# Gated mix of sliding-window attention and a SwiGLU feed-forward: one feed-forward tile by block products instead of two, a new deal of slots, and V's first quarter in another order

## The chip, the core and the metric

The kernel runs on one core of a Trainium2 chip. The metric is the device time of one launch in microseconds (us). The core's engines work side by side, each through its own list of instructions: TensorE (PE in the profile, with its weight loads as PEld), VectorE (DVE), ScalarE (ACT), GpSimd (POOL) and SyncE (SP), which issues most of the transfers (DMAs).

## What is computed

The input x has 2048 rows of 512 numbers. The output mixes two branches by a gate per row:

```python
g = _sigmoid((x * gate_w).sum(-1, keepdims=True))
a = _A_ref(x, A_wqkv, A_wo)                        # attention, 32 heads of 16, row q sees rows q-255 .. q
b = (_silu(x @ w_gate) * (x @ w_up)) @ w_down      # feed-forward, 1792 hidden columns
return g * a + (1 - g) * b
```

## The kernel before, in words

**Numbers.** Every large product is made with each operand split into a high part and a low part (`split`, L67), and three matmuls stand for one: high x high, high x low, low x high. A matmul has 512 moving columns as a rule. The 512 contraction rows are four slices (k = 0 to 3) of 128, so a sum of 128 x 512 results takes 12 matmuls of 128 rows.

**Stages.** TensorE goes through these in order:

1. *V* (L145 to L286). x arrives in four chunks of 512 rows, each in four slices, on SyncE's queue; the four slices of V's weights on ScalarE's queue. Each slice is split: the high part on ScalarE, the low part on VectorE for x, and for V's weights on VectorE (k = 0) or GpSimd (the others), L173 to L178, with two fills of V's store (`fill_v`, L165) on GpSimd among them. The first four row blocks of V (the first quarter) are made together in four accumulators (`first`, L214): for each k, for each of the four row blocks, the three products of that slice (L215 to L217). The other twelve row blocks follow one by one.
2. *Block products* (L367 to L436). Queries and keys of eight groups of four heads, taken in four pairs of groups, and gate and up of the first `NSF` feed-forward tiles (a tile is 128 of the 1792 hidden columns), one tile a pair. In a pair, the two by two blocks of weights and x are combined by additions so that seven block products do what eight would; for the two halves of the rows that makes 7 x 2 x 6 = 84 matmuls of 128 rows. Query and key results are split and written to DRAM (`xd`), gate and up are written as they are (`raws`, L335). In the last pair the constant rows of the first query and key stores are filled and the first heads' queries and keys are read back (`stack`, L320).
3. *The streams beside attention* (L484 to L841). Gate and up of all the other tiles are made by `stream` (L580): the list `UNITS` (L107) has two units, gate and up, a tile, and each unit has four sums, one a chunk of x. The first unit runs alone with whole matmuls (`whole`, L514: 48 steps, one matmul each). The others run in two *lanes* (`lanes`, L525): each sum's contraction is cut into halves of 64 rows, lane 0 does the upper half of a sum, lane 1 the lower half of it, 18 steps later. A *step* is one half matmul of 64 rows in either lane; the two lanes lie in different row halves of the array. 12 steps is the worth of one sum. A finished sum is copied by ScalarE (`copy_out`, L508) and written to `raws`. When a unit is done, the next weights but one are split (`prepare`, L299: the high part on ScalarE, the low part on GpSimd).
   Attention's own work is cut into *slots*. First come 64 slots with the first score pass of head group 0 and three steps each (L690). Then come 128 *blocks* of four slots (L812): in a slot, one head of the first score pass for a later group (`stage1`, L591: a score matmul of 63 rows, whose masked maximum VectorE takes) and one head of the second pass (`stage2`, L631: a score matmul of 64 rows, its exponential by ScalarE, L644, and the masks on GpSimd), then as many steps as the list `DEAL` (L805) says for that block's place in its round of four blocks, dealt out over the four slots. At the second slot of a round's first block stand the value products of the round before (`av`, L654) and their evacuation (`evacuate`, L669). From block 112 on (the last head group, 16 blocks) there is no first score pass any more, and the second list of `DEAL` counts. There the first two feed-forward tiles are also prepared for the last stage: their gate and up are read back (`tile_load`, L740) and go through `tile_early` (L745) on ScalarE and VectorE, at fixed slots; the down weights are split on VectorE.
4. *The last stage* (L843 on): the down product of the feed-forward branch over 14 tiles and four chunks, with the output product of attention between.

The order on each engine is the order of the program, written out by hand; nothing reorders it. What `later`, `at`, `soft` and `spread` hold is tied to slots (for `soft`, copies of finished sums just before value products are put behind them). The matmuls of the score passes rotate through PSUM banks that VectorE (first pass) or ScalarE (second pass) must have read before; the streams rotate through three banks of their own.

Of the kernel before, what the change touches and what calls it, by code (L numbers as in the profile page):

```python
# [12 lines left out]
ALU = mybir.AluOpType  # L13
# [5 lines left out]
NK = D // P  # L19
# [14 lines left out]
def gated_mix(ctx, tc, xT, xn, wqk, wv, wo, wgu, wd, gw, out):  # L34
# [4 lines left out]
    nc = tc.nc  # L39
# [27 lines left out]
    def split(hi, lo, src, hi_eng, lo_eng):  # L67
        if hi_eng is nc.scalar:
            nc.scalar.copy(hi, src)
        else:  # L70
            hi_eng.tensor_copy(hi, src)
        lo_eng.tensor_tensor(out=lo, in0=src, in1=hi.bitcast(F32), op=ALU.subtract)
# [14 lines left out]
    def run(gen, n=None):  # L87

        while n is None or n > 0:
            if next(gen, run) is run:  # L90
                break
            n = n and n - 1
# [10 lines left out]
    def weights_of(key):  # L103
        return wqk[key[1]] if key[0] == "p" else wgu[key[1], :, key[2]]

    NSF = 2
    UNITS = [("f", f, i) for f in range(NSF, NF) for i in range(2)]  # L107

    psum = ctx.enter_context(tc.tile_pool(name="psum", bufs=1, space=PSUM))
# [2 lines left out]
    def bank(n):  # L112
        names = BANKS[n if isinstance(n, str) else ("pa", "pb", "pc", "pd")[n]]
        names.append(names.pop(0))
        return psum.tile([P, CH], F32, name=names[-1])
# [7 lines left out]
    wvh = vpool.tile([P, NK, D], F32R, name="wvh")  # L123
    wvl = vpool.tile([P, NK, D], F32R, name="wvl")
    vs = [vpool.tile([P, G, 2, VW], F32, name=f"vs{i}") for i in range(2)]

    def pair_fetch(keys):
        raw = wide.tile([P, 4, 2 * P], F32, name="rw")
        for i, key in enumerate(keys):
            nc.sync.dma_start(by_k(raw[:, 2 * i:2 * i + 2].rearrange("p a n -> p (a n)")), weights_of(key))  # L130
        return raw

    def u_tile():
        return wide.tile([P, CH], F32, name="u", bufs=6)
# [6 lines left out]
    def xk(c, k):  # L141
        return halves_of(xraw[2 * c + k // 2])[k % 2]

    wvraw = [u_tile() for _ in range(NK)]
# [6 lines left out]
    PAIRS = [(("p", g), ("p", g + 1)) for g in range(0, G, 2)]  # L151
    PAIRS += [(("f", f, 0), ("f", f, 1)) for f in range(NSF)]
    RW = {0: pair_fetch(PAIRS[0])}
# [11 lines left out]
    def fill_v(t):  # L165
        nc.gpsimd.memset(t, 0.0)
        for i in range(2):
            nc.gpsimd.memset(t[:, :, i, :68].rearrange("p g (j e) -> p g j e", e=17)[:, :, :, DH], 1.0)

    def split_x(c, k):  # L170
        split(xhi[c][:, k], xlo[c][:, k], xk(c, k), nc.scalar, nc.vector)

    for k in range(NK):  # L173
        split_x(0, k)
        split(wvh[:, k], wvl[:, k], wvraw[k], nc.scalar, nc.vector if k == 0 else nc.gpsimd)
        if k == 1:
            fill_v(vs[0])
    fill_v(vs[1])  # L178

    def v_products(b):  # L180
        c, o = divmod(b * P, CH)
        return [(xt[c][:, k, o:o + P], wt[:, k]) for k in range(NK)
                for xt, wt in ((xhi, wvh), (xhi, wvl), (xlo, wvh))]
# [24 lines left out]
    def vproj(b, ps, ks=range(NK)):  # L208
        todo = v_products(b)
        for k in ks:  # L210
            for n in range(3 * k, 3 * k + 3):
                nc.tensor.matmul(ps, *todo[n], start=n == 0, stop=n == 3 * NK - 1)

    first = [bank(n // 2) for n in range(4)]  # L214
    for k in range(NK):  # L215
        for b in range(4):
            vproj(b, first[b], (k,))  # L217
    for c in (1, 2):
# [250 lines left out]
    with ExitStack() as A:  # L469
# [121 lines left out]
        def stage1(g, qb):  # L591

            hf, b = divmod(qb, NB // 2)
            if b == 0:
                MX[g, hf] = sm.tile([P, 4, NB // 2], F32, name="mx")
            q0, k0 = qb * P, max(0, qb - 2) * P
            n = q0 + P - k0
            for hd in range(4):
                pr, j = divmod(hd, 2)
                r = slice(64 * j, 64 * j + 63)  # L600

                ps = bank("pd") if g == 0 and pr else bank("pc")
                nc.tensor.matmul(ps[:, :n], QT[g % 2][pr][r, q0:q0 + P], KT[g % 2][pr][r, k0:k0 + n],  # L603
                                 start=True, stop=True)
                mx = nc.vector.tensor_tensor_reduce(out=ps[:, :n], in0=ps[:, :n], in1=mask[:, 3 * P - n:],  # L605
                                                    scale=1.0, scalar=NEG, op0=ALU.add, op1=ALU.max,
                                                    accum_out=MX[g, hf][:, hd, b:b + 1])
                if g == 0:
                    BEHIND.append(mx)
                yield  # L610
# [76 lines left out]
        first = chain(*(stage1(0, b) for b in range(NB)))  # L687
# [114 lines left out]
            spread(4 * (16 * g + 9) + 3, 1, stack(g + 2, 0))  # L802
            spread(4 * (16 * g + 17) + 1, 1, stack(g + 2, 1))

        DEAL = [[[(hd + 1) * n // 4 - hd * n // 4 for hd in range(4)] for n in deal] for deal in ((5, 9, 8, 8), (8, 8, 8, 8))]  # L805
        DEAL[0][0] = 1, 2, 2, 0
        scores = chain(*(stage1(*divmod(b, NB)) for b in range(NB, G * NB)))
        run(scores, 1)
        for t in range(G * NB + 1):
# [7 lines left out]
            for hd in range(4):  # L817
                k = NOW[0] = NSLOT * t + hd
# [8 lines left out]
                if t < G * NB:  # L827
                    run(steps, DEAL[t >= g7][part][hd])
                if hd == 1 and values:
# [205 lines left out]
```

## Time and profile before

| what | us |
|---|---|
| median of 3 runs | 823.76 (821.94 to 824.28) |
| the profiled execution | 822.11 |
| its span, first to last instruction | 820.4 |
| stages in the profiled execution: block products from | 50.66 |
| the streams from | 164.90 |
| blocks of four slots from | 216.13 |
| the last group of heads (block 112) from | 568.38 |
| the last stage from | 619.46 |

How to read it: the profile shows one execution. A line like L564 is a line of the kernel above: L564 are the half matmuls of the lanes, L603 and L642 the two score passes, L664 the value products, L381 the block products, L212 V. A group or a timeline row names what is written and read (`pa<-xhi,wh`: into a bank of pool pa, from the high part of x and of a weight). A bracket at the end of a row gives the idle time before it and what ended it. Matmuls overlap, so a matmul's length is not its price: the distance between the starts of two that follow each other in the same rows of the array is.

### The profile page before, as it was taken

To read this page: it belongs to the slowest core of one execution; us is meant where nothing else is said; L and a number is where in the kernel's file an instruction comes from. 1 tells how busy PE (TensorE), PEld (TensorE's weight loads), DVE (VectorE), ACT (ScalarE), POOL (GpSimd) and SP (SyncE) were. 2 spreads that over 40 slices of the span, in tenths; PEclk is the share of its full clock that TensorE was granted. 3 is DMA by queue.
4 is the path that set the end of the run, shared out by engine and by line. 5 is a ranking of instruction groups with operands and counts; after the bars stand their busy time and mean duration, and the time that the engine had idled before them with its cause. 6 is when DMAs were issued, how large, how long until landed. Compare 5 with 4: busy or idle time off the path is not lost.

```text
span 820.4 us, 20498 instructions
## 1 busy us (share of the span) xinstructions
PE 812.0 (99%) x7681; PEld 681.0 (83%) x7681; DVE 550.4 (67%) x1425; ACT 470.0 (57%) x956; POOL 402.1 (49%) x715
## 2 busy tenths in 40 slices
PE   9999999999999999999999999999999999999997
PEld 7888888878888888888888888888887888888886
DVE  5675554248877888878888887786576666554652
ACT  7455553312576767767677676776776563435340
POOL 5124442260366666767667576665873205442320
PEclk9999999999999999999999999999999999999999
DMA  8446666385625654566555655352659997878611
GB/s 302 148 156 254 231 231 235 137 268 178 218 85 194 189 179 157 182 213 202 171 167 168 207 188 159 132 170 89 212 191 349 271 287 229 273 226 221 213 52 52
DMA packets 80211, 159.70 MB, mean 195 GB/s; under 512 B 14960, under 2 KB 19440, under 8 KB 80112
## 3 DMA queue, kind: packets, MB, share of 16 engines
q1 hardware_dynamic: 68544, 127.44, 47.5%
q0 software_dynamic: 10992, 29.91, 11.3%
q8 instruction: 60, 0.98, 0.5%
q10 hardware_dynamic: 576, 1.05, 0.4%
q14 instruction: 39, 0.32, 0.1%
HBM read 93.32 MB, written 65.01 MB: 193 GB/s over the span
## 4 chain that ended last, share of the span: by engine, by line
PE 95%; DMA 2%; DVE 1%; ACT 1%; POOL 0%; SPq 0%; issue 0%; DVEq 0%; ACTq 0%
PE pa L564 22%; PE pb L564 10%; PE pd L642 6%; PE pc L664 5%; PE pd L381 4%; PE pb L381 4%; PE pa L381 4%; PE pd L81 3%; PE pc L81 3%; PE pc L83 3%; PE pd L83 3%; PE pc L82 3%; PE pd L82 3%; PE pb L664 2%; PE pc L381 2%; PE pb L83 2%
## 5 line engine op out<-in xcount | busy, mean ns | idle before, releaser
L644 ACT ACTIVATE pt<-pd 128x384 f32<-128x384 f32 (+2 forms) x491 | 223.0, 474 | 43.9 <-PE pd L642 25.6
L605 DVE CUSTOM_DVE_ANT_0 pc<-pc,mask 128x384 f32<-128x384 f32 (+2 forms) x322 | 173.2, 548 | 23.5 <-PE pc L603 9.6
L642 PE MATMUL pd<-q,k 64*128 64x384 f32 (+2 forms) x491 | 167.2, 348 | 1.8 <-ACT pt L644 1.8
L564 PE MATMUL pa<-xhi,wh 64*128 64x512 f32 x492 | 168.5, 395 | 0.0
L564 PE MATMUL pa<-xlo,wh 64*128 64x512 f32 x492 | 167.6, 394 | 0.0
L564 PE MATMUL pa<-xhi,wl 64*128 64x512 f32 x492 | 165.9, 395 | 0.0
L646 POOL TENSOR_SCALAR_AFFINE_SELECT pt<-pt 128x256 f32<-128x256 f32 x256 | 110.9, 434 | 67.9 <-ACT pt L644 62.7
L642 PEld LDWEIGHTS pd<-q,k 64*128 64x128 f32 x491 | 90.8, 185 | 26.1 <-ACT pt L644 9.8
L603 PE MATMUL pc<-k,q 63*128 63x384 f32 (+2 forms) x322 | 106.9, 337 | 0.0
L564 PE MATMUL pb<-xhi,wl 64*128 64x512 f32 x244 | 96.2, 394 | 0.0
L564 PE MATMUL pb<-xhi,wh 64*128 64x512 f32 x244 | 96.2, 394 | 0.0
L564 PE MATMUL pb<-xlo,wh 64*128 64x512 f32 x244 | 96.2, 394 | 0.0
L649 POOL TENSOR_SCALAR_AFFINE_SELECT pt<-pt 128x256 f32<-128x256 f32 x224 | 94.3, 421 | 0.0
L605 DVE CUSTOM_DVE_ANT_0 pb<-pb,mask 128x384 f32<-128x384 f32 (+2 forms) x158 | 86.9, 550 | 6.9 <-PE pb L603 3.0
L564 PEld LDWEIGHTS pa<-xhi,wh 64*128 64x128 f32 x492 | 88.2, 185 | 1.9 <-DVE mx L605 0.5
L564 PEld LDWEIGHTS pa<-xhi,wl 64*128 64x128 f32 x492 | 87.0, 185 | 1.1
L564 PEld LDWEIGHTS pa<-xlo,wh 64*128 64x128 f32 x492 | 86.9, 185 | 0.6
L605 DVE DVE_READ_ACCUMULATOR2_ANT mx<- 128x1 f32 x512 | 72.8, 142 | 0.0
L921 DVE TENSOR_TENSOR sg<-got,sg 128x512 f32<-128x512 f32 x52 | 41.1, 790 | 45.2 <-ACT sg L920 39.4
L664 PE MATMUL pd<-pt,vg 64*32 64x320 f32 (+4 forms) x1184 | 63.1, 346 | 0.0
L603 PEld LDWEIGHTS pc<-k,q 63*128 63x128 f32 x322 | 58.6, 184 | 4.8 <-issue 4.3
L682 POOL TENSOR_TENSOR oe<-oe,ob 128x512 f32<-128x512 f32 (+1 forms) x28 | 35.2, 1256 | 54.5 <-ACT ob L675 51.5
(307 smaller groups left out, 2050.8 us busy)
## 6 DMA issues: line engine op xcount, KB each, us to landing
got<-raws SPq DMA_DIRECT2D x104, 256.0 KB
raws<-ev SPq DMA_DIRECT2D x91, 256.0 KB
q<-xd SPq DMA_DIRECT2D x96, 128.0 KB
k<-xd SPq DMA_DIRECT2D x96, 128.0 KB
xd<-cx SPq DMA_DIRECT2D x16, 512.0 KB
xd<-cy SPq DMA_DIRECT2D x16, 512.0 KB
od<-oe POOLq DMA_DIRECT2D x32, 256.0 KB, 3.4
raw<-wgu SPq DMA_DIRECT2D x25, 256.0 KB
```

What stands on the lines that cost most here:

```text
L81: nc.tensor.matmul(ps, lh, rh, start=start and i == 0, stop=False, skip_group_check=skip)
L82: nc.tensor.matmul(ps, lh, rl, start=False, stop=False, skip_group_check=skip)
L83: nc.tensor.matmul(ps, ll, rh, start=False, stop=stop and i == n - 1, skip_group_check=skip)
L381: nc.tensor.matmul(ps, l[:, w], r[:, k], start=n in (1, 2, 5) and k == m == 0, stop=k == 1 and m == 2, skip_group_check=True)
L564: mm = nc.tensor.matmul(ps[o], w[r], x[r], start=first and i == 0, stop=(o is odd or bool(lane)) and i == turn - 1)
L603: nc.tensor.matmul(ps[:, :n], QT[g % 2][pr][r, q0:q0 + P], KT[g % 2][pr][r, k0:k0 + n], start=True, stop=True)
L605: mx = nc.vector.tensor_tensor_reduce(out=ps[:, :n], in0=ps[:, :n], in1=mask[:, 3 * P - n:], scale=1.0, scalar=NEG, op0=ALU.add, op1=ALU.m ...
L642: nc.tensor.matmul(ps[:, :n], KT[g % 2][pr][r, k0:k0 + P], QT[g % 2][pr][r, k0:k0 + n], start=True, stop=True)
L644: BEHIND.append(nc.scalar.activation(pt[:, j, :n], ps[:, :n], AF.Exp, scale=SCALE))
L646: nc.gpsimd.affine_select(out=pt[:, :, :P], in_=pt[:, :, :P], pattern=[[0, 2], [1, P]], compare_op=ALU.is_ge, fill=0.0, base=0, channel_mu ...
L649: nc.gpsimd.affine_select(out=pt[:, :, 2 * P:], in_=pt[:, :, 2 * P:], pattern=[[0, 2], [-1, P]], compare_op=ALU.is_ge, fill=0.0, base=-1, ...
L664: nc.tensor.matmul(AV[g, c][h][32 * j:32 * j + 32, q0 - c * CH:q1 - c * CH], VG[4 * g + kb // 4][o, kb % 4, 17 * j:17 * j + 32], PT[g, kb, ...
```

## The change

Three edits. (a) `NSF` goes from 2 to 1: the second feed-forward tile leaves the block products, and its gate and up become two more units at the head of the streams. (b) The deal of steps to blocks goes from 5, 9, 8, 8 to 5, 10, 9, 9 in a round, and in the last head group from 8, 8, 8, 8 to 9, 9, 9, 8. Inside a block of n steps the slot h gets (h+1)n//4 - hn//4 steps: 8 is 2, 2, 2, 2; 9 is 2, 2, 2, 3; 10 is 2, 3, 2, 3. The 5 stays at 1, 2, 2, 0. (c) In V's first quarter, the first slice's weights are split by VectorE alone, ahead of everything else on it, and the first slice's products are ordered by kind: high x high for the four row blocks, then high x low, then low x high. The other slices keep their order.

```diff
-    NSF = 2
+    NSF = 1
     UNITS = [("f", f, i) for f in range(NSF, NF) for i in range(2)]
...
+    nc.vector.tensor_copy(wvh[:, 0], wvraw[0])
+    nc.vector.tensor_tensor(out=wvl[:, 0], in0=wvraw[0], in1=wvh[:, 0], op=ALU.subtract)
     for k in range(NK):
         split_x(0, k)
-        split(wvh[:, k], wvl[:, k], wvraw[k], nc.scalar, nc.vector if k == 0 else nc.gpsimd)
+        if k:
+            split(wvh[:, k], wvl[:, k], wvraw[k], nc.scalar, nc.gpsimd)
         if k == 1:
             fill_v(vs[0])
     fill_v(vs[1])
...
     first = [bank(n // 2) for n in range(4)]
-    for k in range(NK):
+    for n in range(3):
+        for b in range(4):
+            nc.tensor.matmul(first[b], *v_products(b)[n], start=n == 0, stop=False)
+    for k in range(1, NK):
         for b in range(4):
             vproj(b, first[b], (k,))
...
-        DEAL = [[[(hd + 1) * n // 4 - hd * n // 4 for hd in range(4)] for n in deal] for deal in ((5, 9, 8, 8), (8, 8, 8, 8))]
+        DEAL = [[[(hd + 1) * n // 4 - hd * n // 4 for hd in range(4)] for n in deal] for deal in ((5, 10, 9, 9), (9, 9, 9, 8))]
         DEAL[0][0] = 1, 2, 2, 0
```

## The prediction

> **What bounds the kernel now.** I read the page first: busy shares, then the chain that ended last.
>
> ```profile
> span 820.4 us, 20498 instructions
> PE 812.0 (99%) x7681; PEld 681.0 (83%) x7681; DVE 550.4 (67%) x1425; ACT 470.0 (57%) x956; POOL 402.1 (49%) x715
> PE 95%; DMA 2%; DVE 1%; ACT 1%; POOL 0%; SPq 0%; issue 0%; DVEq 0%; ACTq 0%
> ```
>
> TensorE holds 95% of the chain, so the question is what it issues and how densely. A busy share of 99% doesn't prove density, because matmuls overlap (each lasts 0.39 us in the rows below, longer than the distance to the next). So I went by starts: the chain in order of time, then the timeline.
>
> ```profile
> 145.86 1.36 PE pa L381 x6
> ...
> 164.90 5.44 PE pa L518 x24
> ...
> 179.14 1.39 PE pa L564 x12
> ```
>
> The first row is the start of the last pair of block products (a feed-forward tile), the second the start of the streams. A pair takes 164.90 - 145.86 = 19.04 us; 6 matmuls take 1.36 us, 227 ns each, and 84 x 0.2267 = 19.04. So no gap hides in a pair. The last row is the stream: 12 half matmuls, six steps of one per lane, in 1.39 us, or **0.232 us a step**.
>
> Next I took the stretch in which the stream runs beside attention, a round of four blocks (dealt 5, 9, 8, 8 steps; the first three are shown) cut at the first exponential score of each block:
>
> ```profile
> 391.02:395.85 4.83, 4.83 (x118) 3.30 (x115) 3.41 (x12) 2.06 (x5) 2.22 (x6) 1.00 0.11 34
> 395.85:398.78 2.93, 2.93 (x30) 2.69 (x29) 2.86 (x12) 2.71 (x6) 2.62 (x5) 1.00 0.37 106
> 398.78:401.33 2.55, 2.55 (x28) 2.37 (x25) 2.29 (x7) 2.04 (x5) 1.94 (x6) 1.00 1.02 340
> ```
>
> Columns: length, then busy time of PE, weight loads, DVE, ACT, POOL; clock 1.00 throughout. The third block has 8 steps and, per row half, 4 score matmuls. Steps take 8 x 0.232 = 1.86 us, which leaves 0.69 us for the four scores of a half, 0.17 each. So this block is full of matmuls: DVE (2.29) and ACT (2.04) both finish inside it. The first block carries the value products, and its surplus lies around them, where the change deals no step.
>
> The last group, without the first score pass, is looser. Its blocks of 8 steps (matmuls of L564 alone in the second number):
>
> ```profile
> 575.79:577.98 2.19, 2.19 (x19) 1.00 0.99 239
> ...
> 601.22:604.67 3.45, 2.45 (x19) 1.00 0.27 101
> ```
>
> 2.19 us is the full block (1.86 plus two scores a half). The other loses time, and so does the last block; the timeline says where:
>
> ```profile
> 601.22 0.33 PE L642 MATMUL pb<-q,k 64*128 64x384 f32 x1
> 602.53 0.44 PE L642 MATMUL pd<-q,k 64*128 64x384 f32 x1 [0.99 <-ACT pt L644]
> ...
> 615.35 0.22 PE L642 MATMUL pb<-q,k 64*128 64x128 f32 x1
> 616.18 0.32 PE L642 MATMUL pd<-q,k 64*128 64x128 f32 x1 [0.61 <-ACT pt L644]
> ```
>
> Two score matmuls wait for ScalarE to empty their bank. By starts, less the 0.17 us that a score takes, they cost 1.14 and 0.66 us: 1.8 us together.
>
> **What leaves: one pair.** 84 matmuls, back to back, on the path: **-19.04 us**. VectorE's sums and ScalarE's copies of the pair lay beside them and go unpaid. The pair's eight 256 KB writes of gate and up become eight writes from the stream, the weights' bytes stay the same, so SyncE's queue carries as many issues, only later. What moves closer: the last query and key writes now end one pair before the first scores instead of two. They are issued by the second product of the feed-forward pair, some 16 us ahead of the stream, so I take 0. Two writes still on the way would be the bound: 512 KB each at the 222 GB/s of a pair's stretch (last column) are some 5 us.
>
> ```profile
> 126.82:145.86 19.04, 19.04 (x86) 15.77 (x85) 8.97 (x15) 6.34 (x11) 1.99 (x2) 1.00 0.61 222
> ```
>
> **What comes: two units of the stream.** Gate and up of tile 1 over four chunks are 8 sums of 12 steps: 96 steps. 7 products do the work of 8, so 84 full matmuls are replaced by 96 pairs of halves, and a pair of halves costs 232 ns against 227 for a full one. The deal places them: 28 rounds get 3 more (84, in the second to fourth block), the last group's four rounds 3 more (12, in the first to third). The stream needs 1254 of 1256 dealt steps, as it needed 1158 of 1160, so nothing is left over at the end.
>
> The 84: their blocks are full of matmuls, so each costs its own time. The lower bound is 0.232 us. The upper one comes from the only slot with three steps, the last of the second block:
>
> ```profile
> 397.86 0.37 PE L642 MATMUL pd<-q,k 64*128 64x384 f32 x1
> 398.08 0.39 PE L564 MATMUL pa<-xhi,wl 64*128 64x512 f32 x1
> 398.14 0.39 PE L564 MATMUL pb<-xhi,wh 64*128 64x512 f32 x1
> ...
> 398.78 0.33 PE L642 MATMUL pd<-q,k 64*128 64x384 f32 x1
> ...
> 399.41 0.34 PE L642 MATMUL pd<-q,k 64*128 64x384 f32 x1
> ```
>
> That slot takes 398.78 - 397.86 = 0.92 us, the two-step slot behind it 0.63: 0.29 for the third step. I take 0.24, near the plain steps, because the block of 8 above, with the same two scores in each slot, shows no surplus: 84 x 0.24 = **+20.2 us** (19.5 to 24.4).
>
> The 12: 12 x 0.232 = **+2.8 us**. But they give ScalarE, VectorE and the DMAs time against the two waits above. Their causes:
>
> ```profile
> 600.96 0.63 ACT L748 ACTIVATE ev<-k 128x512 f32<-128x512 f32 x1 [0.45 <-DMA k<-raws]
> 601.49 0.60 ACT L69 CAST wh<-raw 128x512 fp32r<-128x512 f32 x1
> ...
> 615.33 0.62 ACT L69 CAST q<-ev 128x512 fp32r<-128x512 f32 x1 [1.01 <-DVE ev L752]
> ```
>
> ScalarE stands 1.01 us at the last one for VectorE's chain, which starts behind the value products of block 124; three more steps lie between, 0.7 us, so its 0.66 us should go. At the first it stands 0.45 us for a load issued one block earlier and does a weight split right behind its use. Counted from the stream's end the split keeps its step, but six more steps now lie behind the value products of block 120, so it falls two slots later and no longer on the load's user. I take most of both, **-1.6 us** of the 1.8; the bounds are 0 and -1.8.
>
> **V's first quarter.** The high half of V's first weights moves from ScalarE, where it stood second, to VectorE. All four blocks then do high x high first, and each low half is wanted later.
>
> ```profile
> 5.66 0.62 ACT L69 CAST wvh<-u 128x512 fp32r<-128x512 f32 x1
> 6.33 0.49 PE L212 MATMUL pa<-wvh,xhi 128*128 128x512 f32 x1 [0.38 <-ACT wvh L69]
> 10.73 1.55 POOL L72 TENSOR_TENSOR wvl<-u,wvh 128x512 fp32r<-128x512 f32 x1
> 12.64 0.39 PE L212 MATMUL pa<-wvl,xhi 128*128 128x512 f32 x1
> 590.79 0.49 DVE L71 CAST q<-ev 128x512 fp32r<-128x512 f32 x1 [3.50 <-DMA ev<-wd]
> ```
>
> The raw weights are there by 5.66, when ScalarE reads them; a copy on VectorE takes 0.49 us (last row, same shape), so the first product starts near 6.15 instead of 6.33. It would gain more by the second, but GpSimd still delivers the third low weights at 10.73 + 1.55 = 12.28, and their first user stood at 12.64 before. So the gain is clipped to about **-0.3 us** (0 to -0.35), and the rest turns into a wait for GpSimd. No loss: VectorE's subtractions come later than before by the copy, but their users by eight products (1.8 us).
>
> **Sum:** -19.04 + 20.2 + 2.8 - 1.6 - 0.3 = **+2.1 us**. The profiled execution took 822.11 us (1.7 outside its span); it becomes 824.2. The median of the runs shown is 823.76, 1.65 above, so I forecast **825.8 us**, 0.25% more. A measurement of this kernel tells about 0.3%, 2.5 us, from no change.
>
> **Rivals.** *The waits stay* (slower). ScalarE's waits in the last group move with the work instead of being filled: the splits, copies and loads keep their distance to the scores. Sum +3.7 us, **827.4**. For it: the work ahead of them is issued by slots, which shift too. Against: the load and VectorE's chain have lengths of their own. 20%.
>
> *Three-step slots stall* (slower). Place: the second to fourth blocks of 28 rounds. Matmuls leave the queue in order, so where both scores of a slot fall on one half, the other half's second step waits behind the first half's first (398.08, then 398.14, above). At 0.29 a step the 84 cost 24.4 us: +6.3 us, **830.0**. It decides from 0.246 us a step, where the sum passes 2.5 us. Against it: a two-step slot alternates halves in the same way and stays at 0.63. 14%. The Trainium skill (TensorE: Matmul & The Clock Gate, Step-by-step) says that matmuls stay in program order and only weight loads are pulled ahead; the starts above agree.
>
> *The steps ride for free* (faster). If attention's blocks had room, the 84 would cost little; fully free the sum is -18.1 us, **805.6**; it decides below 0.186 a step, where the sum falls under -2.5 us. The weight-load share speaks for it at first sight:
>
> ```profile
> 216.13:568.38 352.25, 352.25 (x4943) 299.61 (x4943) 286.58 (x986) 253.54 (x563) 234.69 (x491) 1.00 0.52 168
> ```
>
> Weight loads are busy 299.61 of 352.25 us, 85%. The Trainium skill (Perfetto Trace Analysis, Identifying the Most-Contended Engine) would have headroom judged by that share, not by matmul time; by it 15% would be open, more than the 84 steps need. The trace doesn't agree: the pair quoted above, with a matmul each 227 ns and no gap, has 15.77 of 19.04, 83%. So 85% is full here. 6%, for partial room.
>
> **Chances and range.** Forecast and its neighbours within 0.3%: 60%. Slower by over 0.3%: 20 + 14 = 34%. Faster: 6%. The range reaches from 822.8, two thirds of the way to where steps at 0.186 would put the time (821.3), to 829.3, most of the way to the stalling case.
>
> **What would show it.** Right: streams start near 145.6 instead of 164.90; a third block, now of 9 steps, takes about 2.79 us, a second one, of 10, about 3.17; the waits for ScalarE in the last group are down to a few tenths; V is done 0.3 us sooner. Wrong: third blocks at 2.55 (free) or 2.84 and more (stalls), a wait for the first query and key loads, or long waits of streams for their banks.

## The result, and the profile after

The changed kernel takes 825.62 us (median of 6 runs, 825.23 to 826.15), the kernel before in the same series 822.43 us (6 runs, 821.41 to 824.28): a ratio of 1.0036, 95% interval 1.0022 to 1.0050. It is slower, by 3.2 us or 0.36%, a little more than the 0.3% that the prediction called the limit of what can be told. The profiled executions say the same: 825.23 us against 822.11, spans 823.5 and 820.4.

The page of the changed kernel, the same three lines as before:

```profile
span 823.5 us, 20684 instructions
PE 814.2 (99%) x7789; PEld 690.0 (84%) x7789; DVE 546.0 (66%) x1413; ACT 469.8 (57%) x954; POOL 404.6 (49%) x717
PE 96%; ACT 2%; POOL 1%; issue 0%; DVE 0%; DVEq 0%; ACTq 0%; POOLq 0%
```

TensorE still holds the chain, but ScalarE now has 2% of it (1% before) and GpSimd 1%, while the 2% of the DMAs are no longer listed. 108 more matmuls are there: 192 halves came, 84 whole ones went. The chain in order of time gives the borders of the stages (lines behind the edits are six higher than before: L387 block products, L524 the first unit of the streams, L648 the second score pass, L650 its exponentials, L670 the value products, L517 the copies of finished sums):

```profile
50.32 1.36 PE pa L387 x6
...
145.52 5.44 PE pa L524 x24
```

V ends 0.34 us sooner (50.66 before), and the pairs before the streams, five now instead of six, take 145.52 - 50.32 = 95.20 us, 19.04 less. The stretches behind that, first of the changed kernel (64 slots, rounds, last head group, last stage), then the two of before that were not shown yet:

```profile
145.52:196.72 51.20, 51.20 (x396) 43.39 (x395) 34.38 (x130) 10.79 (x19) 15.21 (x16) 1.00 0.75 241
196.72:570.40 373.68, 370.31 (x5111) 321.77 (x5112) 289.30 (x987) 259.00 (x571) 236.66 (x493) 1.00 0.51 165
570.40:623.32 52.92, 52.31 (x784) 42.42 (x781) 28.66 (x39) 39.14 (x90) 40.00 (x81) 1.00 0.58 193
623.32:823.50 200.18, 196.30 (x870) 162.30 (x867) 112.92 (x154) 85.54 (x150) 57.00 (x73) 1.00 0.70 217
```

```profile
164.90:216.13 51.23, 51.23 (x397) 43.30 (x396) 34.39 (x130) 10.80 (x19) 15.20 (x16) 1.00 0.74 240
...
568.38:619.46 51.08, 49.27 (x762) 40.60 (x758) 29.55 (x39) 37.70 (x89) 39.21 (x80) 1.00 0.62 202
619.46:820.40 200.94, 196.40 (x870) 162.26 (x867) 111.75 (x154) 85.75 (x151) 57.00 (x73) 1.00 0.70 215
```

| step of the prediction | forecast us | profiled executions us |
|---|---|---|
| one pair leaves | -19.04 | -19.04 |
| V's first quarter | -0.3 | -0.34 |
| the 64 slots | 0 | -0.03 |
| 84 steps in 28 rounds (352.25 to 373.68) | +20.2 | +21.43 |
| 12 steps in the last group, less what they fill | +1.2 | +1.84 |
| last stage and end | 0 | -0.76 |
| sum | +2.1 | +3.1 |

In the rounds something is new. In the second column of the long stretch, PE's busy time is 370.31 of 373.68 us, where it was 352.25 of 352.25. The waits of TensorE's matmuls in the whole run, of the kernel before and then of the changed one (total, times, longest), show what fills the rest:

```profile
PE pd L642 <- ACT pt L644: 1.8, 3, 1.0
```

```profile
PE pd L648 <- ACT pt L650: 3.4, 9, 0.4
...
PE pc L670 <- POOL pt L652: 0.6, 1, 0.6
```

The nine waits of 0.4 us of the second score pass for ScalarE are not the three of before. They all stand at one place: in nine of the 28 rounds (those that begin at blocks 12, 28, 36, 44, 60, 76, 92, 100, 108; a round is named by its first block here) the slot that gets no step, the fourth of the first block, takes 0.88 to 0.91 us between the starts of its second-pass score and the next; in the other rounds, and in the kernel before, 0.39 (0.33 to 0.41). The round at block 12, ScalarE and then TensorE:

```profile
237.89 0.59 ACT L681 COPY ob<-pd 128x512 f32<-128x512 f32 x1 [2.52 <-PE pd L670]
238.37 0.59 ACT L517 COPY ev<-pa 128x512 f32<-128x512 f32 x1
238.85 0.89 ACT L650 ACTIVATE pt<-pd 128x384 f32<-128x384 f32 x2
```

```profile
238.52 0.44 PE L648 MATMUL pd<-q,k 64*128 64x384 f32 x1
238.62 0.40 PE L609 MATMUL pc<-k,q 63*128 63x384 f32 x1
239.41 0.44 PE L648 MATMUL pd<-q,k 64*128 64x384 f32 x1 [0.38 <-ACT pt L650]
```

ScalarE idles 2.52 us while the value products run, then evacuates them (L681), and right behind that copies a finished sum of the streams (L517). The exponentials start a copy later, 238.85 instead of 238.37, and the next score waits for its bank.

### The profile page after: what moved, and what is told of

Same layout as the page of the kernel before. It is cut to its first block, busy times and chain, and to the rows that moved or that the text cites. A ratio compares the mean times of both kernels' runs of the same rounds, so it can differ in the third digit from the quotient of the medians.

```text
span 823.5 us, 20684 instructions
## 1 busy us (share of the span) xinstructions
PE 814.2 (99%) x7789; PEld 690.0 (84%) x7789; DVE 546.0 (66%) x1413; ACT 469.8 (57%) x954; POOL 404.6 (49%) x717
## 4 chain that ended last, share of the span: by engine, by line
PE 96%; ACT 2%; POOL 1%; issue 0%; DVE 0%; DVEq 0%; ACTq 0%; POOLq 0%
PE pa L570 24%; PE pb L570 12%; PE pd L648 7%; PE pc L670 5%; PE pd L387 3%; PE pb L387 3%; PE pa L387 3%; PE pd L81 3%; PE pc L81 3%; PE pc L82 3%; PE pd L82 3%; PE pc L83 3%; PE pd L83 3%; PE pb L670 2%; PE pb L81 2%; PE pb L83 2%
## 5 line engine op out<-in xcount | busy, mean ns | idle before, releaser
L650 ACT ACTIVATE pt<-pd 128x384 f32<-128x384 f32 (+2 forms) x491 | 223.6, 474 | 55.1 <-PE pd L648 36.8
L570 PE MATMUL pa<-xhi,wh 64*128 64x512 f32 x536 | 182.4, 395 | 0.0
L570 PE MATMUL pa<-xlo,wh 64*128 64x512 f32 x536 | 179.7, 391 | 0.0
L570 PE MATMUL pa<-xhi,wl 64*128 64x512 f32 x536 | 179.3, 392 | 0.0
L648 PE MATMUL pd<-q,k 64*128 64x384 f32 (+2 forms) x491 | 166.0, 345 | 3.4 <-ACT pt L650 3.4
L648 PEld LDWEIGHTS pd<-q,k 64*128 64x128 f32 x491 | 90.5, 186 | 21.9 <-ACT pt L650 10.2
L570 PE MATMUL pb<-xhi,wh 64*128 64x512 f32 x264 | 104.0, 394 | 0.0
L570 PE MATMUL pb<-xlo,wh 64*128 64x512 f32 x264 | 103.6, 392 | 0.0
L570 PE MATMUL pb<-xhi,wl 64*128 64x512 f32 x264 | 103.4, 392 | 0.0
L570 PEld LDWEIGHTS pa<-xhi,wh 64*128 64x128 f32 x536 | 96.0, 185 | 2.7 <-DVE mx L611 0.5
L570 PEld LDWEIGHTS pa<-xhi,wl 64*128 64x128 f32 x536 | 93.9, 184 | 1.4
L570 PEld LDWEIGHTS pa<-xlo,wh 64*128 64x128 f32 x536 | 94.2, 185 | 0.7
L927 DVE TENSOR_TENSOR sg<-got,sg 128x512 f32<-128x512 f32 x52 | 44.7, 860 | 44.8 <-ACT sg L926 39.6
L670 PE MATMUL pd<-pt,vg 64*32 64x320 f32 (+4 forms) x1184 | 63.1, 346 | 0.0
```

The costliest lines, as they stand in the source:

```text
L570: mm = nc.tensor.matmul(ps[o], w[r], x[r], start=first and i == 0, stop=(o is odd or bool(lane)) and i == turn - 1)
L648: nc.tensor.matmul(ps[:, :n], KT[g % 2][pr][r, k0:k0 + P], QT[g % 2][pr][r, k0:k0 + n], start=True, stop=True)
L650: BEHIND.append(nc.scalar.activation(pt[:, j, :n], ps[:, :n], AF.Exp, scale=SCALE))
L670: nc.tensor.matmul(AV[g, c][h][32 * j:32 * j + 32, q0 - c * CH:q1 - c * CH], VG[4 * g + kb // 4][o, kb % 4, 17 * j:17 * j + 32], PT[g, kb, ...
```

## The experiments

The theory that I formed on this (A): a sum's copy, or the split of new weights, falls by the new deal into the slot of the value products in nine rounds. There it is written behind their evacuation, though `soft` puts such copies ahead of it when they come one or two slots sooner. Walking through the list of steps gives exactly these rounds: with 33 steps a round and 12 a sum, a sum ends in that slot in every fourth round (at blocks 12, 28, ... 108), and a weight split lands there in the rounds at blocks 36 and 100; with 30 a round none does. The rival (B): there is no such place, each of the 84 steps is dearer than a plain one, 21.4 / 84 = 0.255 us.

**after_lull**: the changed kernel, one comparison changed.

```diff
-            if 16 < due < 4 * (G - 1) * NB and due - 3 < k < due:
+            if 16 < due < 4 * (G - 1) * NB and due - 3 < k <= due:
```

> The changed kernel, but a copy of a finished sum (or a weight split) that is due in the very slot of the value products is issued ahead of their evacuation instead of behind it (the condition in soft reads k <= due). Theory A (copies and splits that the new deal puts right behind the value products hold up ScalarE and so the scores): the slot without steps takes 0.39 us in all rounds again instead of 0.88 to 0.91 in nine of them, 9 x 0.49 = 4.4 us less than the changed kernel: about 821.2 us. Theory B (each of the 84 steps is dearer than a plain one, 21.4 / 84 = 0.255 us): the order of one copy changes nothing, 825.6 us, within 1.

Measured: 822.05 us against 823.52 of the kernel before beside it, ratio 0.9982 (0.9972 to 0.9993); span 819.5. That is 0.9 us above the time that theory A gave, in a series whose kernel before was 1.1 us slower too; by the ratios, 1.0036 and 0.9982, the gain is 4.4 us. All 28 slots without a step take 0.39 or 0.40 us (0.33 in the first round). Its stretch of rounds, and the round at block 12 again, ScalarE and TensorE:

```profile
196.78:566.46 369.68, 369.64 (x5112) 321.24 (x5112) 288.66 (x987) 259.99 (x571) 236.05 (x493) 1.00 0.52 167
```

```profile
235.40 0.59 ACT L517 COPY ev<-pa 128x512 f32<-128x512 f32 x1
237.95 0.59 ACT L681 COPY ob<-pd 128x512 f32<-128x512 f32 x1 [1.97 <-PE pd L670]
238.43 1.13 ACT L650 ACTIVATE pt<-pd 128x384 f32<-128x384 f32 x2
```

```profile
238.59 0.44 PE L648 MATMUL pd<-q,k 64*128 64x384 f32 x1
238.69 0.41 PE L609 MATMUL pc<-k,q 63*128 63x384 f32 x1
238.98 0.44 PE L648 MATMUL pd<-q,k 64*128 64x384 f32 x1
```

The copy now stands in ScalarE's pause, the exponentials follow the evacuation, and the stretch is 4.00 us shorter (373.68 to 369.68). A holds, B falls: the same 84 steps cost 369.68 - 352.25 = 17.43 us, **0.207 us a step**. By the starts of the second pass's score matmuls, which give the length of every slot, the three slots of a round that got a step grew by 18.7 us in the 28 rounds, 0.22 a step, and the other slots shrank by 1.3 us. So the step itself is near its plain 0.232, and a part of its time comes back elsewhere.

**before_phase**: the kernel before, same work and deal, two steps moved from the first round to the last head group, so that sums end two steps later in between.

```diff
-                    run(steps, DEAL[t >= g7][part][hd])
+                    run(steps, DEAL[t >= g7][part][hd] + {(1, 3): -2, (113, 0): 1, (113, 1): 1}.get((t, hd), 0))
```

> The kernel before with the same work and the same deal, but two steps are taken from the second block and given back in the last head group, so that sums end two steps later between the two: by the list of steps, in 14 of the 28 rounds one ends in the slot of the value products, where none did. Theory A: each such round loses the time of one copy on ScalarE, 14 x 0.49 = 6.9 us: about 829.3 us, with the slot without steps at 0.88 in 14 rounds. Theory B: no step was added, so it stays at 822.4 us, within 1.

Measured: 830.03 us, ratio 1.0076 (1.0055 to 1.0097). In exactly 14 rounds the slot takes 0.88 us, in the others 0.39. The rounds take 358.52 us instead of 352.25: 6.3 us for 14 copies, 0.45 each. So the wait can be made in the kernel before without a step more.

```profile
216.41:574.93 358.52, 353.60 (x4940) 300.24 (x4939) 288.18 (x986) 252.47 (x563) 234.17 (x491) 1.00 0.51 165
```

```profile
PE pd L642 <- ACT pt L644: 7.0, 17, 1.5
```

17 waits: 14 new ones beside the three known. The profiled span grew by 8.7 us, 2.4 more than the rounds; 0.3 us of it is a later start of the blocks (216.41 instead of 216.13), part of it a longer wait in the last block (the longest is 1.5 us now), the rest I have not followed.

**before_v**: the kernel before with V's order alone (the second and third hunk of the change).

> The kernel before with the new order of V's first quarter alone. My prediction's term: V is done 0.3 us sooner (block products from 50.3 instead of 50.66) because the third slice's low weights from GpSimd end the wait; everything behind keeps its length, so the span is 820.1. A rival says that the start decides: 0.2 us from the first product alone or 0.6 us if GpSimd were no limit.

One run: 821.36 us, span 819.7. The block products start at 50.02 instead of 50.50 by the timeline (50.16 in the changed kernel). The rounds, in which the edit changes nothing, take 352.83 us against 352.25, so two traces can differ by 0.6 us there without a cause in the kernel:

```profile
215.67:568.50 352.83, 352.74 (x4944) 299.74 (x4943) 286.55 (x986) 253.14 (x563) 233.92 (x491) 1.00 0.52 167
```

The start of V differs by more than the effect. Over the twelve kernels, V's first weights are first read between 5.49 and 6.20 us, so I count from that read to the block products. The old order takes 44.84 us, both in before and in before_phase. The new one takes 44.34 in before_v, 44.67 in the changed kernel, and 44.26 to 44.86 in all ten kernels that have it. So V's order was worth 0.5 us here, more than the 0.35 that I had given as its most. In the changed kernel it is 0.17 us by this count, and the other 0.17 of its 0.34 us are an earlier read (5.49 instead of 5.66, where ScalarE had just ended another copy, so the trace doesn't say when the weights had landed). The first products of the changed kernel (L220 are the first slice in the new order, L215 the other slices):

```profile
6.15 1.10 PE L220 MATMUL pa<-wvh,xhi 128*128 128x512 f32 x2
7.09 0.62 PE L220 MATMUL pb<-wvh,xhi 128*128 128x512 f32 x2
...
9.36 0.39 PE L215 MATMUL pa<-wvh,xhi 128*128 128x512 f32 x1
```

The first product starts at 6.15, as forecast, but the first two take 0.94 us by starts where later two take 0.45, so the twelve end at 9.36, not 8.9; why is open (in before_v the twelve take 2.81 us, here 3.21). From there TensorE doesn't get far enough ahead to wait long for GpSimd, the limit that I had named. That limit does show in after_fill_pd3, where the 12 products end at 8.93: a wait of 0.25 us, but for the second slice's low weights and not for the third's.

**after_fill**: as after_lull, and a step a round goes from the second block into the slot that had none.

```diff
-        DEAL = [[[(hd + 1) * n // 4 - hd * n // 4 for hd in range(4)] for n in deal] for deal in ((5, 10, 9, 9), (9, 9, 9, 8))]
-        DEAL[0][0] = 1, 2, 2, 0
+        DEAL = [[[(hd + 1) * n // 4 - hd * n // 4 for hd in range(4)] for n in deal] for deal in ((6, 9, 9, 9), (9, 9, 9, 8))]
+        DEAL[0][0] = 1, 2, 2, 1
```

> As after_lull, and one step of each round moves from the second block into the slot of the first block that had none (deal 6, 9, 9, 9, slots 1, 2, 2, 1). Theory A says that this slot waits for ScalarE (0.39 us where two scores take 0.33 on one half and nothing on the other) and the next slot too (0.75 instead of 0.63), so a step there is free: 28 x 0.23 = 6.4 us less than after_lull at most, I expect 4 to 6, so 815 to 817 us. Theory B, that a step costs its time wherever it stands: the same as after_lull, within 1 us.

Measured: 818.08 us, ratio 0.9935 (0.9916 to 0.9953), span 815.9, 3.6 less than after_lull; a little less than I expected. Its rounds:

```profile
196.88:562.37 365.49, 365.44 (x5112) 316.73 (x5113) 288.16 (x987) 258.26 (x571) 235.26 (x493) 1.00 0.53 169
```

4.19 us less for 28 moved steps, 0.15 each. By starts, the slot that gets the step grows from 0.39 to 0.51 us, the slot behind it shrinks from 0.75 to 0.65, and the slot that gives the step away loses 0.19. So in its new place a step costs 0.12 us in its own slot and 0.02 net, as theory A said of both slots. **after_fill2** moves one more into the same slot (deal 7, 9, 9, 8, slots 1, 2, 2, 2).

> As after_fill with one more step moved into the same slot (deal 7, 9, 9, 8, slots 1, 2, 2, 2). The slot took 0.51 us with one step, where the two scores and a step need about 0.4, so some 0.1 us of it is still a wait for ScalarE: up to 28 x 0.1 = 2.8 us less than after_fill, I expect 1 to 2. If nothing is left free there, the same.

Measured: 817.99 us, ratio 0.9933 (0.9920 to 0.9946), span 816.3: nothing more than after_fill. The slot grows from 0.51 to 0.74 us, the full price of a step, so one step fills the place.

**before_fill, nsf3_fill, nsf0_fill** keep the copy rule, V's order and the filled slot, and change how many tiles go through block products: two, three, none (after_fill: one). The edit of before_fill against after_fill follows; with NSF at 3 the deal is 6, 7, 7, 7 and 8, 7, 7, 7, with NSF at 0 it is 6, 10, 10, 10 and 10, 10, 10, 8.

```diff
-    NSF = 1
+    NSF = 2
...
-        DEAL = [[[(hd + 1) * n // 4 - hd * n // 4 for hd in range(4)] for n in deal] for deal in ((6, 9, 9, 9), (9, 9, 9, 8))]
+        DEAL = [[[(hd + 1) * n // 4 - hd * n // 4 for hd in range(4)] for n in deal] for deal in ((6, 8, 8, 8), (8, 8, 8, 8))]
```

> Two feed-forward tiles by block products as before, with V's new order, the copy rule of after_lull, and the deal 6, 8, 8, 8 (slots 1, 2, 2, 1): the free slot filled. If a step costs about 0.21 us beside attention (as after_lull against before gives: 17.4 us for 84), 96 steps cost 19.9 us, less what the last group absorbs, against 19.04 us for the pair, and this kernel is within 1 us of after_fill, about 818 us. If a step costs the 0.232 to 0.24 us of my prediction it is 3 us faster than after_fill, 815 us.

> Three tiles by block products, 96 steps fewer than before_fill, deal 6, 7, 7, 7 and 8, 7, 7, 7, filled slot, copy rule and V's order as there. At 0.21 us a step and pairs of 19.04 us again no change of more than 1 us against before_fill; but VectorE needs 0.52 us for a score of the first pass and a round's 16 of them with the evacuation 9 us, so with slots of one and two steps its waits could grow: 0 to 4 us slower. At 0.24 us a step 3 us faster.

> No tile by block products: 96 steps more than after_fill, one pair less (19.04 us); deal 6, 10, 10, 10 and 10, 10, 10, 8, filled slot and copy rule kept. Theory D (a step costs 0.232 us once the scores no longer wait for ScalarE, and less as long as it fills such waits: 0.126 us from 27 to 30 steps a round, 0.173 from 30 to 33): from 33 to 36 few waits are left, so 84 x 0.21 to 0.23 plus about 2.5 in the last group is 20.1 to 21.8 us against 19.04: 1 to 3 us slower than after_fill, 819 to 821. If the price stays at 0.173 it is 2 us faster, 816.

Measured, for two, three and no tiles: 821.32 us (ratio 0.9983, 0.9973 to 0.9994), 827.52 us (1.0053, 1.0040 to 1.0065) and 817.05 us (0.9918, 0.9904 to 0.9931). Their rounds, in the order three, two and no tiles:

```profile
235.26:575.60 340.34, 339.71 (x4776) 272.70 (x4775) 277.10 (x986) 247.69 (x554) 230.16 (x489) 1.00 0.53 168
```

```profile
215.66:566.58 350.92, 350.83 (x4944) 293.44 (x4943) 288.18 (x986) 252.19 (x563) 234.32 (x491) 1.00 0.53 168
```

```profile
179.02:560.10 381.08, 381.08 (x5279) 336.51 (x5280) 287.85 (x987) 263.77 (x580) 238.34 (x495) 1.00 0.52 168
```

And the waits of the second score pass's weight loads for ScalarE in the whole run, in the order three, two, one and no tiles:

```profile
PEld pd L648 <- ACT pt L650: 25.0, 86, 1.0
```

```profile
PEld pd L648 <- ACT pt L650: 16.4, 63, 0.9
```

```profile
PEld pd L648 <- ACT pt L650: 6.3, 27, 0.4
```

```profile
PEld pd L648 <- ACT pt L650: 0.8, 3, 0.3
```

| steps a round | rounds us | price of each of the 84 steps more | of it in the slots that got them | those waits us |
|---|---|---|---|---|
| 27 | 340.34 | | | 25.0 |
| 30 | 350.92 | 0.126 | 0.177 | 16.4 |
| 33 | 365.49 | 0.173 | 0.211 | 6.3 |
| 36 | 381.08 | 0.186 | 0.218 | 0.8 |

The fourth column counts only the slots that got a step, by the starts of the scores; the other slots became shorter, by 4.3, 3.2 and 2.7 us.

The price rises as the waits for ScalarE go, which is the direction of theory D. But the two don't match in size: against 0.232 a step, the 84 came 8.9, 4.9 and 3.9 us cheaper, while the waits fell by 8.6, 10.1 and 5.5. And the price ends at 0.186, below the 0.21 to 0.23 that D gave for the last step of the table, so there D was wrong: nsf0_fill is not 1 to 3 us slower than after_fill but 1.0 us faster by the medians, too little to tell the two apart (the intervals of their ratios overlap). None of my expectations of before_fill held either: it is neither level with after_fill nor faster, but 3.2 us slower by the medians (1.9 by the spans, 817.8 and 815.9, where its profiled execution is the fastest of its eleven). And nsf3_fill is 6.2 us slower than before_fill, more than the 4 I allowed, without the longer waits for VectorE that I had feared. A pair of block products at 19.04 us for 96 steps is 0.198 us a step, and beside attention, with the slot filled, the steps are cheaper than that.

**after_fill_pd3**: as after_fill, with the bank that the first unit hands over going to the second score pass instead of the first.

```diff
-            BANKS["pc"].append("pb1")
+            BANKS["pd"].append("pb1")
...
-                BANKS["pc"].remove("pb1")
-                BANKS["pd"].append("pb1")
+                pass
```

> As after_fill, but the bank that the streams hand over goes to the second score pass (three banks, ScalarE) instead of the first (then two, VectorE). If waits for ScalarE are still worth anything at 33 steps a round, up to 2 us faster; VectorE, which needs 0.52 us a score and copies out behind the value products, then has a bank less, and its waits could cost 0 to 4 us. I expect the second to win: 0 to 3 us slower than after_fill.

Measured: 823.65 us, ratio 1.0006 (0.9995 to 1.0017), 5.6 us more than after_fill and so more than I allowed for. The waits for ScalarE are gone from the head of the list, and in their place stands the first pass, which waits for VectorE's evacuation copy with a bank less:

```profile
PEld pc L609 <- DVE oe L687: 7.4, 27, 0.3
```

So this didn't measure what ScalarE's waits alone are worth: it changed one wait for another. The starts of the scores part the two as far as they can be parted: the slot right behind the value products grows from 0.59 to 0.92 us, 9.2 us in 28 rounds, and everything else in the rounds becomes 2.9 us shorter.

**after_lull_sp**: as after_lull, the last unit's sums written by SyncE instead of GpSimd.

```diff
-            queue = nc.gpsimd if key == UNITS[-1] else nc.sync
+            queue = nc.sync
```

> As after_lull, but the last unit's sums are written by SyncE instead of GpSimd. In the changed kernel the last value product waits 0.6 us for a mask that stands on GpSimd behind three issues of transfers. Theory C (this wait took the place of ScalarE's in the last group): the wait goes, the last block takes 4.6 us instead of 5.2, the span 0.6 us less. Rival: the mask was held by VectorE's chain through another issue in front of it, and nothing changes.

One run: 822.67 us, span 821.0. The last block and the last stage, of after_lull and then of this kernel:

```profile
614.09:619.31 5.22, 4.62 (x108) 2.96 (x106) 3.63 (x6) 3.91 (x8) 4.95 (x11) 1.00 0.88 246
619.31:819.50 200.19, 196.29 (x870) 162.35 (x867) 112.96 (x154) 85.50 (x150) 57.32 (x73) 1.00 0.68 218
```

```profile
614.06:618.41 4.35, 4.34 (x109) 2.86 (x105) 2.88 (x5) 3.86 (x8) 4.09 (x8) 1.00 0.80 210
618.41:821.00 202.59, 196.99 (x870) 162.13 (x867) 113.69 (x154) 85.90 (x151) 56.79 (x72) 1.00 0.70 216
```

Theory C holds for the block, 0.87 us shorter and without the wait. But the last stage gets 2.4 us longer, with two new waits of TensorE for VectorE in it:

```profile
PE pd L83 <- DVE hl L72: 1.2, 2, 0.9
```

So the gain is more than given back: the span is 1.5 us longer than after_lull's, not 0.6 shorter, in this one run. In the last stage ScalarE now stands 1.83 us at 621.66 for a read-back of gate and up (`q<-raws`), which SyncE issues behind one of the moved writes; after_lull has no such wait there. That this read-back is late because of the write was not tried.

## Why the prediction was right, point by point

The forecast of 825.8 us and its range held the time, and the sign was right. But a part of this is luck. The sum came out near the measured one with two terms wrong in opposite ways: the steps cost 2.8 us less than forecast, and a term that I had not seen cost 4.0. The time itself lies within 0.2 us because the kernel before, from whose 823.76 us I counted, took 822.43 in the series: the rise was 3.2 us, not 2.1. And the measured 0.36% lies just over the bound inside which I had put 60% of the chances; the case that came is the one with 34%, though neither of its two mechanisms came.

*One pair leaves: right.* 19.04 us, nothing appeared in its place, and the 64 slots behind it kept their length: the nearer query and key writes cost nothing.

*The 84 steps: the sum was nearly right, the step behind it wrong.* I took 0.24 us a step. The price is 0.207 (after_lull against before), which makes 17.4 us, 2.8 less than forecast. That the blocks were full of matmuls I had shown with one block, a third one. Over the 28 rounds of the changed kernel the third blocks did grow by 0.24 us (2.50 to 2.74), as forecast. The second and fourth grew by 0.18 and 0.19: their added steps cost 0.22 and 0.21 in their own slots, but the slot that had three steps before shrank from 0.90 to 0.85, and the first slot of the fourth block from 0.68 to 0.64. The blocks that I said would show it read so, second and third of the round at block 56:

```profile
386.75:389.85 3.10, 3.10 (x30) 2.98 (x30) 2.93 (x12) 2.49 (x6) 2.79 (x6) 1.00 0.39 104
389.85:392.60 2.75, 2.75 (x28) 2.71 (x27) 2.46 (x9) 2.26 (x5) 1.83 (x5) 1.00 0.96 349
```

3.10 and 2.75 us, forecast 3.17 and 2.79. Waits of the score matmuls' weight loads for ScalarE shrink as steps are added. That these are what the added steps fill is argued from the four kernels above, and their sizes don't match one to one; no kernel changes these waits alone.

*What the prediction missed.* I wrote that the first block's surplus lies "where the change deals no step" and left it out. The block got no step, but it got the end of sums and two weight splits: 4.0 us in nine rounds. The deal sets two things, how many steps stand in a block and where each sum ends, and I only followed the second one in the last head group. Both it and the copy rule stood in the code.

*The last group: direction right, size wrong.* ScalarE's two waits of before are gone as forecast, and no wait of TensorE for ScalarE is left there. But 1.84 us came instead of 1.2. One wait moved on: the last value product now waits 0.61 us for a mask that stands behind GpSimd's issues of transfers. And the larger of the two waits of before was not wholly the deal's: in before_v, whose last group has the same deal, ScalarE doesn't stand for the load at all, the score waits 0.41 us instead of 0.99, and the block takes 2.88 us instead of 3.45. So some 0.6 us of the gain depends on when a load lands.

```profile
622.87 0.53 PE L670 MATMUL pc<-pt,vg 64*32 64x64 f32 x22 [0.61 <-POOL pt L652]
```

```profile
621.47 0.42 POOL L652 TENSOR_SCALAR_AFFINE_SELECT pt<-pt 128x256 f32<-128x256 f32 x1
621.82 0.56 POOL L518 DMA_DIRECT2D raws<-ev  x1
622.39 0.42 POOL L652 TENSOR_SCALAR_AFFINE_SELECT pt<-pt 128x256 f32<-128x256 f32 x1
```

after_lull_sp shows that taking the issue away takes this wait away. So of the 1.6 us that I took off, about 1.0 came (2.8 less 1.84), and the new wait is about as long as the rest.

*V's first quarter: right in size, in part by luck.* V's start alone differs by 0.7 us from trace to trace, and before_v gained 0.5 us. What held the gain down in the changed kernel was the slow first two products, not GpSimd, as before_v's section says.

*The rivals.* "The waits stay" did not come as told: they went, and others came elsewhere. "Three-step slots stall" is refuted: a third step adds 0.21 to 0.22 us in the changed kernel (slots of three take 0.84 to 0.87 in the mean, the same slots with two steps before 0.62 to 0.65), not 0.29; what I read from one slot before was that slot's own wait. "The steps ride for free" was too far, but its direction counted: 0.207 is under the plain 0.232, and in the slot without steps a step costs 0.02 net. Weight loads at 85% were not full everywhere: with no tile by block products they are busy 336.51 of 381.08 us, 88%.

*Open.* The last stage with the end behind it is 0.76 us shorter in the changed kernel, and again in after_lull (200.19 us); I did not forecast it, and its cause is open.

## What to carry to other kernels

When work is dealt over slots, changing how much stands in a slot also shifts where each piece ends, and what is issued at its end (a copy, a split) meets other work: list these ends against the places where that engine is already late, before counting the price of the work. Put such a copy into the engine's pause (here, the 2.5 us in which value products run) instead of behind it: one comparison gave 4.0 us, more than the whole change moved. And read the price of added work from a place like the one it goes to; with the copy rule and the filled slot, the versions with one tile or none by block products, 0.9935 and 0.9918 of the time before, beat both kernels of this study and the same versions with two tiles (0.9983) and three (1.0053), probably because work that fills waits for another engine is cheaper than its own duration.

## What the runs showed of the hardware that I had not expected

A step in each lane (a pair of half matmuls) costs 0.232 us in a stretch of its own, but 0.207 us on average when added between score matmuls, and 0.126 us where the scores' weight loads wait for ScalarE the most (27 to 30 steps a round). A bank moved from the first score pass to the second (after_fill_pd3) cost more than 6 us in the rounds (365.49 to 371.83), though VectorE's busy time there is 293.60 of 371.83 us:

```profile
196.88:568.71 371.83, 371.11 (x5113) 329.25 (x5112) 293.60 (x989) 258.85 (x571) 236.20 (x493) 1.00 0.51 166
```
